# Block 1's mean and rate transposed inside a feature tile, block 2's two slots later, and block 3's statistics behind block 2's normalisation

## The chip, the cores and the metric

The kernel runs on one core of a Trainium2 chip. The metric is the device time of one execution, in microseconds (us); three executions are timed and their median counts. One further view, the profile, shows one of these executions instruction by instruction.

## The reference

The function takes x of 2048 rows and 512 columns, normalises every row, feeds the normalised rows to a 32-head attention and to a gated feed-forward network, and joins the two:

```python
def _layernorm(x, axis=-1, eps=1e-5):
    m = jnp.mean(x, axis=axis, keepdims=True)
    v = jnp.var(x, axis=axis, keepdims=True)
    return (x - m) / jnp.sqrt(v + eps)

def reference(A_x, A_wqkv, A_wo, B_x, B_w_gate, B_w_up, B_w_down):
    x = A_x
    xn = _layernorm(x, axis=-1)
    s = _A_ref(xn, A_wqkv, A_wo)                      # softmax attention, 32 heads of 16
    g = _silu(_B_ref(xn, B_w_gate, B_w_up, B_w_down)) # (silu(xn @ w_gate) * (xn @ w_up)) @ w_down
    return x + s * g
```

The change touches only the part that produces xn and its products with wqkv.

## The kernel before, in words

The 2048 rows are worked in four blocks (0 to 3) of 512 rows. The first 141.9 us are a prologue: xn of each block is made, split into two float32r halves (`hi` and `lo`, the tiles `xt`), and multiplied with wqkv. Then the attention runs with the feed-forward network's matmuls filled in between, to the end.

**Slots.** The prologue's matmuls are an explicit list of 48 slots, twelve to a block: slot number = 12 * block + position. A slot is one product tile of 12 matmuls on TensorE (PE). Eight slots of a block are *feature tiles* (`feature_tile`, line 770: queries and keys, 128 features by 512 rows), four are *value tiles* (`value_tile`, line 789). In blocks 0 and 1 the value tiles come first, in blocks 2 and 3 last. So slots 4 to 11 are block 0's feature tiles, 12 to 15 block 1's value tiles, 16 to 23 block 1's feature tiles, 24 to 31 block 2's feature tiles, 32 to 35 its value tiles, and block 3 begins at slot 36. A feature tile ends with a Square on ACT (line 775, into `sq`), a copy on ACT that rounds the high half (line 776, into `parts`), a subtraction on DVE for the low half (line 777), a store of 512 KB from SP (line 779) and, from block 1 on, a running maximum on DVE (line 781, `top`). The product's PSUM tile `ps` has four buffers, `parts` four and `sq` two.

**The normalised columns of blocks 1 to 3.** Block 0 is transposed by PE. The others are loaded twice: as rows for the statistics, and as columns (the transposed x, `A_x_columns`) for the normalisation. What has to be done for block b is cut into steps by `columns_of` (line 681), and each step is hung on a slot. The eight numbers of a call at lines 829 to 831 are the slots of: the load of the rows; the load of the columns (`turned`); the statistics (`counted`: BN_STATS and BN_AGGR, one pair per 128 rows; all four in one slot for block 1, two in each of two slots for blocks 2 and 3); the rate (`rated`: `rates_x`, nine small DVE operations and a square root on ACT that fill the tile `mr` with mean and rate); the transposition of `mr` (`spread`); the read of the result (`read`); the normalisation (`normed`: subtract and multiply on DVE with `wide_mr`, a rounding copy on ACT for `hi`); and the offsets of the low halves (`lows`).

`spread_mr` (line 673) is a chain over three engines: PE transposes `mr` into the PSUM tile `extra` (line 674), ACT copies it to SBUF (line 675), and ACT issues a DMA that writes the 4 KB to `mr_d` in HBM (line 676). `load_mr` (line 678) is the DMA from POOL's queue that reads `mr_d` and spreads it over all 128 partitions as `wide_mr` (512 KB). `store_x` (line 656) is a pair of 1 MB stores of a block's `xt` from POOL.

Nothing reorders the instructions: each engine takes them in the order in which the program writes them, and it waits at the first one whose inputs are not there. Steps of a slot marked 0 are written ahead of the slot's matmuls, those marked 1 behind its tile. The loop at line 837 calls `run_steps` for both.

`project` (line 711) writes the 12 matmuls of a tile, for each of four chunks c of the contraction: `hi` with the high weights, `lo` with the high weights, `hi` with the low weights. An `order` list may put another piece of work between them: an entry whose second part is `None` is called instead.

Of the kernel before, what the change touches and what calls it, by code (L numbers as in the profile page):

```python
# [28 lines left out]
DT = D // P  # L29
# [90 lines left out]
def tile_block(ctx: ExitStack, tc: tile.TileContext, x, xcols, wqkv, wo, w_gate, w_up, w_down, out):  # L120
# [401 lines left out]
    with ExitStack() as pro:  # L522
# [10 lines left out]
        xin = facc  # L533
# [15 lines left out]
        wh = pc.tile([P, 8, DT, P], F32R, name="wh")  # L549
        wl = pc.tile([P, 8, DT, P], F32R, name="wl")  # L550
# [51 lines left out]
        raw_x = pc.tile([P, DT, TB], F32, name="raw_x")  # L602
# [59 lines left out]
        def step(at, late, make, *what):  # L662
            steps.setdefault((at, late), []).append(partial(make, *what))
# [17 lines left out]
        def columns_of(b, rows, cols, ats):  # L681
            load, turned, counted, rated, spread, read, normed, lows = ats
            block = slice(b * TB, (b + 1) * TB)
            step(load, 0, sp.dma_start, rows, x[block].rearrange("(t p) d -> p t d", p=P))
            step(turned, 0, sp.dma_start, cols, xcols[:, block].rearrange("(c p) t -> p c t", p=P))
            for t in range(NT):
                step(counted + (t // 2 if b > 1 else 0), 0, stats, t, rows)
            step(rated, 0, rates_x)
            step(spread, 0, spread_mr, b)
            step(read, 1, load_mr, b)  # L690
            hi, lo = xt[b % 2]
            for t in range(NT if b == 1 else 0):
                of = slice(t * P, (t + 1) * P)
                raw = cols[:, :, of]
                step(normed + t + 1, 0, dve.tensor_sub, lo[:, :, of], raw, hi[:, :, of].bitcast(F32))
            for t in range(NT if b == 1 else 0):
                of = slice(t * P, (t + 1) * P)
                raw = cols[:, :, of]
                for i, change in enumerate((dve.tensor_sub, dve.tensor_mul)):
                    step(normed + t, 0, change, raw, raw, wide_mr[:, i, of][:, None].to_broadcast([P, DT, P]))  # L700
                step(normed + t, 1, nc.scalar.copy, hi[:, :, of], raw)
            for c in range(DT if b > 1 else 0):
                raw = cols[:, c]
                step(normed + c, 0, dve.tensor_sub, raw, raw, wide_mr[:, 0])
                step(normed + c, 0, dve.tensor_mul, raw, raw, wide_mr[:, 1])
                step(normed + c, 1, nc.scalar.copy, hi[:, c], raw)
                step(normed + lows[c], 1, dve.tensor_sub, lo[:, c], raw, hi[:, c].bitcast(F32))
            step(normed + lows[-1], 1, store_x, b)


        def project(pairs, xh, xl, tokens, order=None, ps=None):
            ps = ps or pps.tile([P, 512], F32, tag="ps", name="ps")
            n = 0
            terms = [((xh, whi), (xl, whi), (xh, wlo)) for whi, wlo, _ in pairs]
            for i, part in order or [(i, slice(0, 3)) for i in range(DT)]:
                if part is None:
                    i()
                    continue
                c = pairs[i][2]
                for a, w in terms[i][part]:  # L720
                    if tokens is None:
                        mm(ps, w, a[:, c], start=n == 0, stop=n == 3 * DT - 1)
                    else:
                        mm(ps, a[:, c, tokens], w, start=n == 0, stop=n == 3 * DT - 1)
                    n += 1
            return ps
# [42 lines left out]

        def feature_tile(b, m):  # L770
            xh, xl = xt[b % 2]
            ps = project([(wh[:, m, c], wl[:, m, c], c) for c in range(DT)], xh, xl, None)
            parts = p3.tile([P, 2, TB], F32R, tag="parts", name="parts")
            sq = p5.tile([P, TB], BF, tag="sq", name="sq") if b else top[m]
            act(sq, ps, AF.Square)
            nc.scalar.copy(parts[:, 0], ps)
            dve.tensor_sub(parts[:, 1], ps, parts[:, 0].bitcast(F32))
            dst = (q_d if m < 4 else k_d)[:, (m % 4) * P:(m % 4 + 1) * P, b * TB:(b + 1) * TB]
            sp.dma_start(dst.rearrange("s f t -> f s t"), parts.bitcast(F32))
            if b:  # L780
                dve.tensor_max(top[m], top[m], sq)
# [40 lines left out]
        def copy_fx(i):  # L822
# [4 lines left out]
            nc.scalar.copy(dst[:, 2 * w:2 * w + 2], xt[0][j][halves[u], 2 * w:2 * w + 2])  # L827

        columns_of(1, raw_x, xin, (1, 2, 2, 3, 5, 5, 9, (NT + 1,)))
        columns_of(2, raw_x, raw_x, (4, 11, 7, 9, 11, 14, 19, (1, 2, 3, 3)))  # L830
        columns_of(3, xin, raw_x, (16, 24, 17, 24, 26, 26, 31, (1, 2, 3, 3)))

        for b in range(NB):
            more = b + 1 < NB
            slots = [(feature_tile, m) for m in range(8)]
            slots = [(value_tile, t) for t in range(NT)] + slots if b < 2 else slots + [(value_tile, t) for t in range(NT)]
            for n, (make, i) in enumerate(slots):
# [60 lines left out]
        with tc.If(fast < 1):  # L898
            with tc.tile_pool(name="gen", bufs=1) as gen:
                for h in range(2):  # L900
                    pool.memset(qst[0][h * HALF:h * HALF + 2].bitcast(F32), 0.0)
                for g in range(NG):
                    for b in range(NB):
# [3 lines left out]
                        for j in range(NB):  # L907
                            load_k(g, j, j % 2)
                            for i in range(4 * NT):
                                h, t = divmod(i, NT)  # L910
                                ps = pps.tile([P, 512], F32, tag="ps", name="ps")
# [42 lines left out]
    for u in range(units):  # L954
        g, b = divmod(u, NB)
# [153 lines left out]
```

## Time and profile before

| | us |
|---|---|
| median of 3 executions (lowest, highest) | 1386.54 (1385.94, 1386.88) |
| the profiled execution's own time | 1385.94 |
| its span in the profile | 1384.2 |
| PE busy in the span | 1375.8 (99%) |
| ACT, DVE, POOL busy | 1157.0, 777.8, 104.7 |
| PE busy in the first 125 us | 121.46 |

The profiled execution took 1385.94 us by the clock that times all executions; 1384.2 us of that is the span from the first to the last instruction, and 1.74 us lie around it. A timeline row gives the start, the duration, the engine, the line, the operation with its output and input, and in square brackets how long the engine sat idle before and what released it. PEld is the weight load of PE; ACTq and SPq are DMA issues by those engines. Matmuls overlap: a row's duration is longer than the distance to the next matmul.

### The profile page before, as it was taken

Reading aid. Unit: us, or ns where it says so; the run is one execution under the profiler, and the core shown is the slowest. Engines: PE = TensorE matmul, PEld = TensorE weight load, DVE = VectorE, ACT = ScalarE, POOL = GpSimd, SP = SyncE. Lnnn points to the kernel's source line nnn. Section 1 sums busy time; section 2 is a strip of 40 time slices with the busy share of each in tenths; the row PEclk is TensorE's granted clock in tenths of the full one; section 3 lists DMA queues with packets and bytes.
Section 4 is the critical chain, followed back from the end, with each engine's and each line's share of the span. In section 5 each row is a group of like instructions: output and inputs, shape, how many; then the busy total and the mean of one; then the engine's idle time right before and its main releaser. Section 6 shows DMA issues by size and latency. Waiting matters only on the chain.

```text
span 1384.2 us, 27644 instructions
## 1 busy us (share of the span) xinstructions
PE 1375.8 (99%) x11152; PEld 866.4 (63%) x11152; DVE 777.8 (56%) x1256; ACT 1157.0 (84%) x1944; POOL 104.7 (8%) x148
## 2 busy tenths in 40 slices
PE   9999999999999999999999999999999999999998
PEld 7777666556655665565566555566566656656565
DVE  6565466365545663565465643655466545655656
ACT  6743589888888898899998988888888888899875
POOL 4300100000010000000110000000100000000142
PEclk9999999999999999999999999999999999999999
DMA  9889541124453511233724402256333312234752
GB/s 289 298 293 289 146 108 44 36 73 109 110 128 82 135 43 36 51 90 87 175 55 110 114 13 51 74 128 143 85 77 84 100 28 57 59 87 135 226 184 85
DMA packets 132900, 156.29 MB, mean 113 GB/s; under 512 B 13481, under 2 KB 83137, under 8 KB 131998
## 3 DMA queue, kind: packets, MB, share of 16 engines
q1 hardware_dynamic: 124974, 128.03, 35.5%
q0 software_dynamic: 7312, 25.89, 5.4%
q8 instruction: 89, 1.46, 0.4%
q10 hardware_dynamic: 480, 0.54, 0.1%
q14 instruction: 45, 0.37, 0.1%
HBM read 112.18 MB, written 40.12 MB: 110 GB/s over the span
## 4 chain that ended last, share of the span: by engine, by line
PE 89%; DVE 0%; DVEq 0%; issue 0%
PE acc L450 33%; PE bankx L244 30%; PE score L990 10%; PE single L990 8%; PE banky L244 6%; PE spare L990 1%; PE spare L1045 0%; PE banky L1045 0%; PE score L1045 0%; DVE y L1052 0%; PE single L1045 0%; DVE y L1058 0%; DVEq L1105 0%
## 5 line engine op out<-in xcount | busy, mean ns | idle before, releaser
L450 PE MATMUL acc<-pr,vst 128*17 128x512 f32 x4096 | 459.3, 593 | 0.0
L1000 ACT ACTIVATE pr<-single 128x512 f32<-128x512 f32 x762 | 429.4, 605 | 17.5 <-PE single L990 0.5
L993 ACT ACTIVATE pr<-score 128x1024 f32<-128x1024 f32 x318 | 327.9, 1031 | 87.5 <-PE score L990 84.6
L244 PE MATMUL bankx<-fx,guh 64*128 64x512 f32 x896 | 290.9, 392 | 0.1
L244 PE MATMUL banky<-fx,guh 64*128 64x512 f32 x896 | 290.9, 392 | 0.0
L450 PEld LDWEIGHTS acc<-pr,vst 128*17 128x17 f32 x4096 | 115.6, 97 | 279.4 <-issue 275.3
L997 DVE COPY pr<-spare 128x512 f32<-128x512 f32 x194 | 134.0, 691 | 183.4 <-PE spare L990 168.5
L990 PE MATMUL score<-qst,kst 50*128 50x512 f32 x830 | 218.6, 418 | 0.0
L990 PE MATMUL single<-qst,kst 50*128 50x512 f32 x922 | 212.4, 398 | 0.0
L244 PE MATMUL bankx<-wd,hh 64*128 64x512 f32 x672 | 196.0, 391 | 0.0
L244 PE MATMUL banky<-wd,hh 64*128 64x512 f32 x672 | 196.0, 391 | 0.0
L1010 ACT ACTIVATE pr<-pr 128x512 f32<-128x512 f32 x354 | 193.3, 641 | 0.0
L244 PEld LDWEIGHTS bankx<-fx,guh 64*128 64x128 f32 x896 | 166.8, 186 | 21.1 <-DVE guh L205 0.6
L244 PE MATMUL banky<-fx,gul 64*128 64x512 f32 x448 | 175.6, 392 | 0.0
L244 PE MATMUL bankx<-fx,gul 64*128 64x512 f32 x448 | 175.6, 392 | 0.0
L990 PEld LDWEIGHTS score<-qst,kst 50*128 50x128 f32 x830 | 98.7, 184 | 112.5 <-ACT pr L1000 68.8
L244 PEld LDWEIGHTS banky<-fx,guh 64*128 64x128 f32 x896 | 166.9, 186 | 0.4
L1000 ACT ACTIVATE pr<-score 128x512 f32<-128x512 f32 x194 | 117.0, 603 | 35.6 <-PE spare L990 26.7
L997 DVE COPY pr<-single 128x512 f32<-128x512 f32 x160 | 110.4, 690 | 58.8 <-PE single L990 47.8
L244 PEld LDWEIGHTS bankx<-wd,hh 64*128 64x128 f32 x672 | 125.1, 186 | 18.4
L990 PEld LDWEIGHTS single<-qst,kst 50*128 50x128 f32 x922 | 114.7, 184 | 23.5 <-ACT pr L1000 7.6
L244 PEld LDWEIGHTS banky<-wd,hh 64*128 64x128 f32 x672 | 125.1, 186 | 5.7
(195 smaller groups left out, 1688.9 us busy)
## 6 DMA issues: line engine op xcount, KB each, us to landing
gur<-in_B_w_gate_dram SPq DMA_DIRECT2D x56, 256.0 KB
gur<-in_B_w_up_dram SPq DMA_DIRECT2D x56, 256.0 KB
wdr<-in_B_w_down_dram SPq DMA_DIRECT2D x56, 256.0 KB
kst<-k_d SPq DMA_DIRECT2D x192, 64.0 KB
qst<-q_d SPq DMA_DIRECT2D x192, 64.0 KB
fx<-xt_d SPq DMA_DIRECT2D x24, 512.0 KB
q_d<-parts SPq DMA_DIRECT2D x16, 512.0 KB
k_d<-parts SPq DMA_DIRECT2D x16, 512.0 KB
```

Source lines behind the costliest of these rows:

```text
L244: mm(bank, lhs[h], rhs[h], start=start, stop=stop)
L450: mm(acc[h * 32:h * 32 + DH + 1], v[:, kt % CT, h * (DH + 1):(h + 1) * (DH + 1)], probs[2 * i + h // 2][:, h % 2], start=kt == 0, stop=kt ...
L990: mm(banked[h], k[r, j, kc * P:(kc + 1) * P], q[r, j], start=True, stop=True)
L993: exps.append(act(pr, both_banks, AF.Exp, scale=0.25))
L997: dve.tensor_copy(pr[:, h], banked[h])
L1000: exps.append(act(pr[:, h], banked[h], AF.Exp, scale=0.25))
L1010: exps.append(act(part, part, AF.Exp, scale=0.25))
```

## The change

Three edits, in four lines of the table and two functions. Block 1's `spread_mr` is no longer called ahead of slot 5 but from inside that slot's feature tile (block 0, m = 1), behind two of its four chunks, which is six matmuls later. Block 2's `spread_mr` goes from slot 11 to slot 13, and the read of its result from slot 14 to slot 13. For block 3 the load of the rows goes from slot 16 to 18, the statistics from slots 17 and 18 to 23 and 24, the rate from 24 to 25, and transposition and read from 26 to 27. Sizes and counts of all instructions stay the same.

```diff
             step(rated, 0, rates_x)
-            step(spread, 0, spread_mr, b)
+            if b > 1:
+                step(spread, 0, spread_mr, b)
             step(read, 1, load_mr, b)
...
         def feature_tile(b, m):
             xh, xl = xt[b % 2]
-            ps = project([(wh[:, m, c], wl[:, m, c], c) for c in range(DT)], xh, xl, None)
+            order = [(c, slice(0, 3)) for c in range(DT)]
+            if (b, m) == (0, 1):
+                order.insert(2, (partial(spread_mr, 1), None))
+            ps = project([(wh[:, m, c], wl[:, m, c], c) for c in range(DT)], xh, xl, None, order)
...
-        columns_of(2, raw_x, raw_x, (4, 11, 7, 9, 11, 14, 19, (1, 2, 3, 3)))
-        columns_of(3, xin, raw_x, (16, 24, 17, 24, 26, 26, 31, (1, 2, 3, 3)))
+        columns_of(2, raw_x, raw_x, (4, 11, 7, 9, 13, 13, 19, (1, 2, 3, 3)))
+        columns_of(3, xin, raw_x, (18, 24, 23, 25, 27, 27, 31, (1, 2, 3, 3)))
```

The diff adds a line and then three more, so line 777 of before is line 781 of after, and so on. In the rows that follow, `xt_167` and `xt_168` are the high and low halves of blocks 0 and 2, `xt_169` and `xt_170` those of blocks 1 and 3.

PE at the start of slot 11, before: the transposition of block 2's mean and rate stands ahead of the last feature tile of block 0.

```order
L722 MATMUL ps<-xt_168,wh 128x512
L722 MATMUL ps<-xt_167,wl 128x512
L674 MATMUL extra<-ident,mr 8x128
L722 MATMUL ps<-xt_167,wh 128x512
L722 MATMUL ps<-xt_168,wh 128x512
```

PE after, at the start of slot 13:

```order
L725 MATMUL ps<-vh,xt_170 128x512
L725 MATMUL ps<-vl,xt_169 128x512
L674 MATMUL extra<-ident,mr 8x128
L725 MATMUL ps<-vh,xt_169 128x512
L725 MATMUL ps<-vh,xt_170 128x512
```

It moved by 24 matmuls, and now stands between two value tiles of block 1.

POOL behind the last weight split, before (`kst` and `qst` are attention tiles that get a constant; slots 11 to 15):

```order
L881 MEMSET qst_566 2x1024 x2
L658 DMA xt_d<-xt_169 128x2048
L658 DMA xt_d<-xt_170 128x2048
L679 DMA wide_mr<-mr_d 128x1024
L785 DMA v_d<-vt 128x8x272
```

POOL after:

```order
L885 MEMSET qst_563 2x1024 x2
L679 DMA wide_mr<-mr_d 128x1024
L658 DMA xt_d<-xt_169 128x2048
L658 DMA xt_d<-xt_170 128x2048
L789 DMA v_d<-vt 128x8x272
```

The load of block 2's mean and rate went ahead of the two 1 MB stores of block 1's xn.

DVE in slots 17 to 19, before: two pairs of block 3's statistics (from `facc`, where its rows lie) stand ahead of block 2's first normalisation (`raw_x` with `wide_mr`); two more pairs stand just above.

```order
L777 TENSOR_TENSOR parts<-ps,parts 128x512
L781 TENSOR_TENSOR top_155<-top_155,sq 128x512
L611 BN_STATS st<-facc 128x6
L612 BN_AGGR mv<-st 128x2
L611 BN_STATS st<-facc 128x6
L612 BN_AGGR mv<-st 128x2
L777 TENSOR_TENSOR parts<-ps,parts 128x512
L781 TENSOR_TENSOR top_156<-top_156,sq 128x512
L667 TENSOR_TENSOR raw_x<-raw_x,wide_mr 128x512 x2
```

DVE after, in slots 22 and 23:

```order
L781 TENSOR_TENSOR parts<-ps,parts 128x512
L785 TENSOR_TENSOR top_160<-top_160,sq 128x512
L667 TENSOR_TENSOR xt_168<-raw_x,xt_167 128x512 x2
L611 BN_STATS st<-facc 128x6
L612 BN_AGGR mv<-st 128x2
L611 BN_STATS st<-facc 128x6
L612 BN_AGGR mv<-st 128x2
L781 TENSOR_TENSOR parts<-ps,parts 128x512
L785 TENSOR_TENSOR top_161<-top_161,sq 128x512
```

The statistics now stand behind the last two low halves of block 2 (`xt_168<-raw_x,xt_167`).

## The prediction

> **What bounds the kernel now.** First the page: its busy table says which engine to look at. Then the waits of PE over the whole span, and PE's timeline around the two that matter.
>
> ```profile
> span 1384.2 us, 27644 instructions
> ...
> PE 1375.8 (99%) x11152; PEld 866.4 (63%) x11152; DVE 777.8 (56%) x1256; ACT 1157.0 (84%) x1944; POOL 104.7 (8%) x148
> ```
>
> ```profile
> PE extra L674 <- DVE mr L629: 1.4, 1, 1.4
> ...
> PE ps L722 <- DVE xt L667: 1.0, 1, 1.0
> ```
>
> ```profile
> 39.66 0.40 PE L722 MATMUL ps<-xt,wl 128*128 128x512 f32 x1
> 41.45 0.27 PE L674 MATMUL extra<-ident,mr 128*8 128x128 f32 x1 [1.40 <-DVE mr L629]
> ...
> 44.35 0.63 PE L724 MATMUL ps<-vh,xt 128*128 128x512 f32 x2
> ...
> 77.95 0.63 PE L722 MATMUL ps<-xt,wh 128*128 128x512 f32 x2
> ...
> 78.65 0.63 PE L722 MATMUL ps<-xt,wh 128*128 128x512 f32 x2
> ...
> 79.35 0.40 PE L722 MATMUL ps<-xt,wh 128*128 128x512 f32 x1
> 80.79 0.50 PE L722 MATMUL ps<-xt,wh 128*128 128x512 f32 x1 [1.05 <-DVE xt L667]
> ```
>
> PE is busy 99% of the span: what keeps it waiting is paid in full, and other engines' work counts only where PE waits for it. The list of PE's waits has one more row, at the kernel's opening, which the change leaves alone. The two shown are in its reach: the transposition of block 2's `mr` at slot 11, and block 2's first feature tile (slot 24, from 77.95), which stops for a low half.
>
> The distance between matmuls gives their true price. Three take 78.65 - 77.95 = 0.70 us, one 0.233. Slot 12 starts at 44.35 and slot 24 at 77.95, so a slot is 33.60 / 12 = 2.80 us. At slot 11 the transposition was due at 39.66 + 0.23 = 39.89 and came at 41.45: **1.56 us lost**. In slot 24 the matmul due at 79.35 + 0.23 = 79.58 came at 80.79: **1.21 us lost**. Together 2.77.
>
> **Part 1, block 1's transposition inside slot 5.**
>
> ```profile
> 23.05 0.27 PE L674 MATMUL extra<-ident,mr 128*8 128x128 f32 x1
> ```
>
> ```profile
> 24.73 0.25 ACT L675 COPY busy<-extra 8x128 f32<-8x128 f32 x1
> 25.01 0.59 ACTq L676 DMA_DIRECT2D mr_d<-busy  x1
> ```
>
> ```profile
> 36.81 1.42 DVE L667 TENSOR_TENSOR facc<-facc,wide_mr 128x512 f32<-128x512 f32 x2 [0.49 <-DMA wide_mr<-mr_d]
> ```
>
> PE had no idle time here in before, and the transposition costs it the same in the new place: six matmuls (1.40) later, at about 24.5, ending near 24.8. ACT came to it only at 24.73, so the chain slips by 0.1 us or so. DVE waits for that chain (0.49 at 36.81) and hands the slip on. Cost on PE: between 0 and 0.1, taken as 0, with part 2's spare as cover.
>
> **Part 2, block 2's transposition at slot 13.** The 1.56 goes: `mr` is done just before 41.45, and PE reaches slot 13 two slots later. What is late next is block 1's own low halves, which PE now wants 1.56 earlier.
>
> ```profile
> 41.92 0.68 DVE L667 TENSOR_TENSOR xt<-facc,xt 128x512 fp32r<-128x512 f32 x1
> ...
> 47.92 0.69 DVE L667 TENSOR_TENSOR xt<-facc,xt 128x512 fp32r<-128x512 f32 x1 [0.68 <-ACT xt L667]
> ...
> 50.63 0.69 DVE L667 TENSOR_TENSOR xt<-facc,xt 128x512 fp32r<-128x512 f32 x1 [0.69 <-ACT xt L667]
> ```
>
> ```profile
> 44.49 0.25 ACT L675 COPY busy<-extra 8x128 f32<-8x128 f32 x1
> 44.77 0.28 ACTq L676 DMA_DIRECT2D mr_d<-busy  x1
> 45.09 0.60 ACT L775 ACTIVATE top<-ps 128x512 bf16<-128x512 f32 x1 [0.35 <-ACT busy L675]
> ```
>
> Slot 12 starts at 44.35 - 1.56 = 42.79; its second matmul, at 43.02, reads the first low half, done at 41.92 + 0.68 = 42.60. Slot 14 (48.39, its second matmul 48.62) reads the third, done at 48.61 in before; slot 15 (51.19, 51.42) the fourth, done at 51.32. Before both, DVE waited for ACT, and on ACT the copy and the DMA issue of `mr` (44.49 to 45.09, 0.6 us) now stand behind that work. So they come at about 48.0 and 50.7: spare 0.4, 0.6 and 0.7 us. If ACT gives nothing back it is 0.4, 0.0 and 0.1. New wait: 0 to 0.4, taken as 0.1.
>
> On POOL the load of `wide_mr` now waits for `mr_d` ahead of two 1 MB stores.
>
> ```profile
> 29.78 0.57 POOL L679 DMA_DIRECT2D wide_mr<-mr_d  x1 [3.57 <-DMA mr_d<-busy]
> ```
>
> ```profile
> 86.34 0.27 ACTq L676 DMA_DIRECT2D mr_d<-busy  x1
> ```
>
> ```profile
> 93.65 0.54 POOL L679 DMA_DIRECT2D wide_mr<-mr_d  x1 [11.48 <-DMA mr_d<-busy]
> ```
>
> ```profile
> DMA to landing us min/median/max: 7.0/7.1/12.0
> ```
>
> ACT's issue of `mr_d` now stands behind block 1's last high half (for which DVE waited until 50.63), at about 50.1. The first hop took 29.78 - 25.01 = 4.8 for block 1 and 93.65 - 86.34 = 7.3 us for block 3; the second, in the row of landings (the transfers of `wide_mr`), 7.0 to 12.0. So `wide_mr` lands between 50.1 + 4.8 + 7.0 = 61.9 and 50.1 + 7.3 + 12.0 = 69.4. The 12.0 must be block 2's, which stood behind 2 MB of stores: block 1's was read at 36.81 and block 3's at 102.75, each less than 10 us from its issue. Now it goes ahead, so I take the low end, 62. The stores wait a few us longer; nothing in the prologue reads them.
>
> [...]
>
> **Part 3, block 3's statistics behind block 2's normalisation.**
>
> ```profile
> 51.34 0.37 SPq L667 DMA_DIRECT2D facc<-in_A_x_dram  x1
> ```
>
> ```profile
> 59.65 0.69 DVE L777 TENSOR_TENSOR parts<-ps,parts 128x512 fp32r<-128x512 f32 x1 [8.34 <-ACT parts L776]
> ...
> 64.73 0.69 DVE L611 BATCH_NORM_STATS2 st<-facc 128x6 f32<-128x512 f32 x1 [4.06 <-DMA facc<-in_A_x_dram]
> ...
> 65.56 0.66 DVE L611 BATCH_NORM_STATS2 st<-facc 128x6 f32<-128x512 f32 x1
> ...
> 69.81 1.41 DVE L667 TENSOR_TENSOR raw_x<-raw_x,wide_mr 128x512 f32<-128x512 f32 x2
> ...
> 77.80 1.41 DVE L667 TENSOR_TENSOR raw_x<-raw_x,wide_mr 128x512 f32<-128x512 f32 x2
> 79.12 0.68 DVE L777 TENSOR_TENSOR parts<-ps,parts 128x512 fp32r<-128x512 f32 x1
> ...
> 80.06 1.28 DVE L667 TENSOR_TENSOR xt<-raw_x,xt 128x512 fp32r<-128x512 f32 x2
> ...
> 82.19 0.16 DVE L670 COPY mr<-mv 128x4 f32<-128x4 f32 x1
> ...
> 83.39 0.17 DVE L629 SCALAR_TENSOR_TENSOR mr<-nw,mr 128x4 f32<-128x4 f32 x1
> ...
> 102.75 1.41 DVE L667 TENSOR_TENSOR raw_x<-raw_x,wide_mr 128x512 f32<-128x512 f32 x2
> ...
> 111.50 0.69 DVE L667 TENSOR_TENSOR xt<-raw_x,xt 128x512 fp32r<-128x512 f32 x1 [0.61 <-ACT xt L667]
> ```
>
> ```profile
> 48.00:64.00 16.00, 16.00 (x71) 12.86 (x70) 3.62 (x6) 10.76 (x15) 2.53 (x4) 1.00 1.01 363
> 64.00:80.00 16.00, 15.74 (x68) 12.34 (x66) 14.99 (x30) 10.83 (x18) 0.00 (x0) 1.00 0.60 226
> ```
>
> DVE stood 4.06 us at block 3's rows and from there hardly paused (14.99 busy in the 16 us from 64, the third busy figure) until the low half that PE waited for: slot 24's stall comes from there. Four pairs of statistics (65.56 - 64.73 = 0.83 each, 3.3 us) and the wait for their rows leave the way. Block 2's normalisation is then bound by its slot. Tile 16's subtraction came at 59.65, 1.3 us after slot 17 began (44.35 + 5 x 2.80); tile 18's so comes at 62.4 + 1.3 = 63.7, and with its maximum DVE is free at 64.6. Four normalisations (79.12 - 77.80 = 1.32), four tiles' subtraction and maximum (80.06 - 79.12 = 0.94) and four low halves (0.64) make 11.6 us, and some 1.1 of waiting for tiles 19 and 20: done at 77.3. Slot 24 starts at 76.39 and wants the last two low halves at 78.0 and 78.7: 1.2 us or more of spare, so 1.21 is gained.
>
> The statistics follow: four pairs (3.3), two tiles (1.9) and the rate (83.56 - 82.19 = 1.4) give `mr` at 83.9; slot 27 wants it at 76.39 + 8.40 = 84.8. The rows' load is issued near 62, behind tile 17's store, and took 13.4 us in before (51.34 to 64.73): 75.5, in time for 77.3. DMA engines were full from 48 to 64 and 60% busy from 64 to 80 (the last figure but one), so this megabyte, some 3 us at 363 GB/s, fits. Block 3's chain, a slot later on a PE 2.77 earlier, keeps the old 86.3 and lands at 86.3 + 7.3 + 7.1 = 100.7. From 102.75 to the last low half's end are 9.4 us, 0.6 of it a wait that shortens with PE; slot 36 (77.95 + 1.21 + 33.60 - 2.77 = 110.0) wants that half at 112.4. So the normalisation may start as late as 103.6. Cost 0, with 1 to 3 us of cover.
>
> **Sum.** 1.56 + 1.21 - 0.1 = 2.67 us off the profiled execution: 1385.94 - 2.67 = 1383.27. It was the fastest of three, the median is 0.60 above. The removed waits hang on transfers and PE's other work hardly waits, so part of the 0.60 is likely these waits grown longer; I take half: 1386.54 - 2.67 - 0.30 = **1383.6**. With 0.4 of new wait and none of the 0.60 it is 1384.2; with no new wait and all of it 1383.2, and 0.4 of scatter (half of the three runs' 0.94) below that 1382.8. A measurement of this kernel can tell about 0.2%, 2.77 us, from no change: a line at 1383.77, just above the forecast.
>
> **The rivals.**
> *Block 1's low halves take the wait's place* at slots 12 to 15. For it: spare of 0.4, none if DVE's chain slips. Against: ACT's shorter queue. A slip of 1 us gives 1384.3.
> *Block 2's mean and rate land too late.* DVE has 1.1 us of waits and 1.2 behind them, so a landing after 66.9 stops slot 24. At the upper end, 69.4, that is 2.5 us: gain 0.5, 1386.1. Against: the load now stands first.
> *Block 3 becomes the stop* (slower). The same two hops, DMA engines full, at slot 36: from a normalisation start of 103.6 PE pays one for one. Both hops at 12.0 give 86.3 + 24.0 + 0.5 = 110.8, 7.2 us, less the 2.94 gained: 1390.8. It is slower than before from 106.5. Against: in before that load was read at 102.75 without a wait.
> *The edits do nothing*, because another product of DVE is as late at both places: 1386.5. No row shows one.
>
> **How the numbers follow.** Forecast 0.66, block 1's halves 0.11, block 2 late 0.08, block 3 late 0.13, nothing 0.02. About three quarters of the forecast lie below 1383.77, as its sum was made from the fastest execution: faster 0.49. Same: 0.17 + 0.11 + 0.08 + 0.02 = 0.38. Slower 0.13. The range 1382.8 to 1386.3 leaves out block 3 late and the last case; the forecast's own is 1382.8 to 1384.2.
>
> **What would show it.** Right: L674 without idle time at slot 13; no PE wait for `xt` near 78; no DVE wait for block 3's rows. Wrong: a PE wait between 42 and 52, DVE waiting for `wide_mr` past 66.9, or PE waiting for `mr` near 85 or for `xt` near 110 to 113.

## The result, and the profile after

The changed kernel took 1383.37 us (median of 12 executions, 1382.67 to 1385.37) against 1386.63 (12 executions, 1385.72 to 1388.81) of the kernel before: 3.26 us less, a ratio of 0.9976 with a 95% interval of 0.9968 to 0.9985. The forecast was 1383.6, the range 1382.8 to 1386.3. Run again beside three of the experiments it was 2.46 us faster (0.9982, 0.9973 to 0.9991).

The page's head and the list of PE's waits after the change (us in total, times, longest):

```profile
span 1382.0 us, 27647 instructions
...
PE 1375.3 (100%) x11152; PEld 866.1 (63%) x11152; DVE 777.8 (56%) x1256; ACT 1157.3 (84%) x1944; POOL 105.1 (8%) x148
```

```profile
PE extra L579 <- DVE ind L586: 1.1, 1, 1.1
PE acc L639 <- DVE xn L737: 0.5, 1, 0.5
PE ps L761 <- DMA wraw<-in_A_wqkv_dram: 0.2, 1, 0.2
```

Both waits in the change's reach are gone; the three rows left belong to the opening (before 8.2 us). PE's busy time did not shrink (1375.8 to 1375.3): the span is shorter by idle time alone. This execution's opening was slower than that of the profile before: PE was busy 18.18 us of its first 20 against 18.90, so the rows below stand about 0.45 us late for a reason outside the change. From slot 9 on they stand about 0.75 us late: slot 8 lost another 0.3 us, which part 1 below comes back to.

PE's timeline at the transposition of slot 13, and at slot 24, which starts at 77.09:

```profile
46.00 0.39 PE L725 MATMUL ps<-vl,xt 128*128 128x512 f32 x1
46.23 0.27 PE L674 MATMUL extra<-ident,mr 128*8 128x128 f32 x1
...
77.09 0.63 PE L723 MATMUL ps<-xt,wh 128*128 128x512 f32 x2
...
78.49 0.63 PE L723 MATMUL ps<-xt,wh 128*128 128x512 f32 x2
...
79.19 0.63 PE L723 MATMUL ps<-xt,wh 128*128 128x512 f32 x2
```

The transposition follows its predecessor by the usual 0.23. In slot 24 chunks three and four (78.49 and 79.19) come at the pace of 0.70 per three matmuls. DVE, ACT, POOL and SP, which set what PE finds:

```profile
50.43 0.69 DVE L667 TENSOR_TENSOR xt<-facc,xt 128x512 fp32r<-128x512 f32 x1 [0.69 <-ACT xt L667]
...
65.38 1.41 DVE L667 TENSOR_TENSOR raw_x<-raw_x,wide_mr 128x512 f32<-128x512 f32 x2
...
77.50 1.29 DVE L667 TENSOR_TENSOR xt<-raw_x,xt 128x512 fp32r<-128x512 f32 x2
78.70 0.69 DVE L611 BATCH_NORM_STATS2 st<-facc 128x6 f32<-128x512 f32 x1
...
84.98 0.16 DVE L629 SCALAR_TENSOR_TENSOR mr<-nw,mr 128x4 f32<-128x4 f32 x1
...
99.31 1.42 DVE L667 TENSOR_TENSOR raw_x<-raw_x,wide_mr 128x512 f32<-128x512 f32 x2 [0.17 <-DMA wide_mr<-mr_d]
```

```profile
50.58 0.27 ACTq L676 DMA_DIRECT2D mr_d<-busy  x1
...
75.94 0.59 ACT L780 CAST parts<-ps 128x512 fp32r<-128x512 f32 x1 [0.79 <-DMA q_d<-parts]
```

```profile
54.65 0.57 POOL L679 DMA_DIRECT2D wide_mr<-mr_d  x1 [9.03 <-DMA mr_d<-busy]
55.21 1.07 POOL L658 DMA_DIRECT2D xt_d<-xt  x2
```

```profile
62.72 1.27 SPq L667 DMA_DIRECT2D facc<-in_A_x_dram  x1
```

And the two windows that the prediction shows of before, now after the change (DMA share is the last figure but one), with the landings of `wide_mr`:

```profile
48.00:64.00 16.00, 16.00 (x70) 12.93 (x69) 4.45 (x8) 11.38 (x18) 2.53 (x4) 1.00 0.81 279
64.00:80.00 16.00, 16.00 (x70) 12.87 (x69) 13.79 (x25) 11.44 (x18) 1.08 (x2) 1.00 1.05 351
```

```profile
DMA to landing us min/median/max: 4.8/6.5/7.0
```

Block 2's normalisation starts at 65.38, 4.4 us earlier than before, and PE no longer overtakes it. Note POOL: it now stands 9.03 us at the load of `wide_mr`, and block 1's two stores of 1 MB leave at 55.21 instead of 50.89. POOL before, for comparison:

```profile
50.89 0.57 POOL L658 DMA_DIRECT2D xt_d<-xt  x1 [5.67 <-ACT xt L667]
51.62 0.53 POOL L658 DMA_DIRECT2D xt_d<-xt  x1 [0.16 <-issue]
52.14 0.53 POOL L679 DMA_DIRECT2D wide_mr<-mr_d  x1
```

The DMA engines' full stretch comes later than before (0.81, then 1.05; before 1.01, then 0.60). The experiments show that the moved stores are more than a side effect.

### The profile page after: what moved, and what is told of

Its sections match the earlier page's. It is cut to its first block, busy times and chain, and to the rows that moved or that the text cites. A ratio compares the mean times of both kernels' runs of the same rounds, so it can differ in the third digit from the quotient of the medians.

```text
span 1382.0 us, 27647 instructions
## 1 busy us (share of the span) xinstructions
PE 1375.3 (100%) x11152; PEld 866.1 (63%) x11152; DVE 777.8 (56%) x1256; ACT 1157.3 (84%) x1944; POOL 105.1 (8%) x148
## 4 chain that ended last, share of the span: by engine, by line
PE 89%; DVE 0%; DVEq 0%; issue 0%
PE acc L450 33%; PE bankx L244 29%; PE score L994 10%; PE single L994 8%; PE banky L244 7%; PE spare L994 1%; PE spare L1049 0%; PE banky L1049 0%; PE single L1049 0%; DVE y L1056 0%; PE score L1049 0%; DVE y L1062 0%; DVEq L1109 0%
```

## The experiments

Each kernel was timed beside the kernel before, in the same session; the times are differences of the medians, with the ratio and its interval.

**1. Block 1's edit alone.**

```diff
-        columns_of(2, raw_x, raw_x, (4, 11, 7, 9, 13, 13, 19, (1, 2, 3, 3)))
-        columns_of(3, xin, raw_x, (18, 24, 23, 25, 27, 27, 31, (1, 2, 3, 3)))
+        columns_of(2, raw_x, raw_x, (4, 11, 7, 9, 11, 14, 19, (1, 2, 3, 3)))
+        columns_of(3, xin, raw_x, (16, 24, 17, 24, 26, 26, 31, (1, 2, 3, 3)))
```

> Only block 1's transposition goes inside slot 5; blocks 2 and 3 as before. Theory: PE had no wait there and the chain behind it slips by 0.1 us, so the time stays within 0.5 us of before, and both PE waits (1.4 and 1.0 us in the list) stay. Rival: the edit shortens block 1's chain by itself and takes over 0.5 us off.

Measured: -0.13 us, 1.0000 (0.9991 to 1.0009). PE's waits in its profile:

```profile
PE ps L723 <- DVE xt L667: 1.4, 1, 1.4
...
PE extra L674 <- DVE mr L629: 0.7, 1, 0.7
```

Both waits are there, 0.7 and 1.4 instead of 1.4 and 1.0. A shorter first stop brings PE to the second one earlier, so the two may trade between executions; two profiles do not show that. The edit is worth nothing that can be measured.

**2. Block 2's edit alone** (the kernel before, with the one line of the table).

```diff
-        columns_of(2, raw_x, raw_x, (4, 11, 7, 9, 11, 14, 19, (1, 2, 3, 3)))
+        columns_of(2, raw_x, raw_x, (4, 11, 7, 9, 13, 13, 19, (1, 2, 3, 3)))
```

> Only block 2's transposition and read go to slot 13. Theory: the wait at slot 11 goes (1.56 us), but slot 24 waits for a chain that is held by the landing of block 3's rows and not by PE, so PE only arrives there earlier and waits 1.2 + 1.5 = about 2.7 us instead of 1.2; the time falls by 0 to 0.8 us. Rival: the two waits are independent and the time falls by 1.4 to 1.8 us with the wait of slot 24 still near 1.2.

Measured: -2.71 us, 0.9983 (0.9974 to 0.9992), and no PE wait on `mr` or `xt`. Both expectations fell: this edit alone gives what all three give, as far as the intervals can tell. Its profile, DVE at block 3's first statistics (still in slot 17) and POOL:

```profile
59.75 0.69 DVE L611 BATCH_NORM_STATS2 st<-facc 128x6 f32<-128x512 f32 x1
```

```profile
56.18 0.57 POOL L679 DMA_DIRECT2D wide_mr<-mr_d  x1 [10.69 <-DMA mr_d<-busy]
56.74 1.06 POOL L658 DMA_DIRECT2D xt_d<-xt  x2
```

DVE does not wait for the rows any more (4.06 us before). Their load was issued at 51.01, as before; what changed is that POOL's two stores, held behind the load of `wide_mr`, left at 56.74 instead of 50.89. That became the new theory, for runs 5 and 6.

**3. Block 3's edit alone** (the kernel before, with the other line).

```diff
-        columns_of(3, xin, raw_x, (16, 24, 17, 24, 26, 26, 31, (1, 2, 3, 3)))
+        columns_of(3, xin, raw_x, (18, 24, 23, 25, 27, 27, 31, (1, 2, 3, 3)))
```

> Only block 3's load, statistics, rate, transposition and read move. Theory: the wait at slot 11 stays at 1.4 to 1.6 us, the one in slot 24 goes; time 1.0 to 1.5 us below before. Rival: the two waits are linked in this direction too and the time hardly falls.

Measured: -1.64 us, 0.9990 (0.9981 to 0.9999). As the theory had it, slot 24's wait is gone and slot 11's stays; the gain is a little over the 1.0 to 1.5 us expected, well within the interval:

```profile
PE extra L674 <- DVE mr L629: 1.6, 1, 1.6
```

**4. Blocks 2 and 3, without the edit inside slot 5** (both lines above in the kernel before).

> Both table edits without the one inside slot 5. Theory: block 1's edit is worth nothing, so the time falls by 2.7 to 3.3 us as in the whole change and no wait for mr or xt is left on PE. Rival: block 1's place matters, a wait between 42 and 52 us shows, and the fall is 0.4 us or more smaller.

Measured: -2.69 us, 0.9983 (0.9974 to 0.9992), no PE wait for `mr` or `xt`. It cannot be told from run 2: on top of block 2's edit, block 3's adds nothing that can be measured, and block 1's neither.

**5. Block 2's transposition moved, its read not** (the kernel before, one number).

```diff
-        columns_of(2, raw_x, raw_x, (4, 11, 7, 9, 11, 14, 19, (1, 2, 3, 3)))
+        columns_of(2, raw_x, raw_x, (4, 11, 7, 9, 13, 14, 19, (1, 2, 3, 3)))
```

> The second edit without its read: block 2's transposition at slot 13, but the load of wide_mr back at slot 14, behind the two 1 MB stores of block 1; the rest as before. Theory now: the second edit also cured slot 24, because its load waits for mr_d ahead of those stores and so keeps them off the DMA engines while block 3's rows come in. With the stores first again (issued near 51 us) the rows land near 64 us, slot 24 waits about 2.7 us, and the time is within 0.8 us of before. Rival: the shorter wait at slot 11 alone lets DVE be in time; then the time is again 2.7 us below before and no wait for xt shows.

Measured: +2.59 us, 1.0017 (1.0008 to 1.0026): slower than before, though slot 11's wait is gone. The mechanism of the theory was there, its time (within 0.8 us) was missed. POOL, SP, DVE and PE in its profile:

```profile
50.19 0.57 POOL L658 DMA_DIRECT2D xt_d<-xt  x1 [5.07 <-ACT busy L675]
```

```profile
50.65 0.37 SPq L667 DMA_DIRECT2D facc<-in_A_x_dram  x1
```

```profile
65.69 0.69 DVE L611 BATCH_NORM_STATS2 st<-facc 128x6 f32<-128x512 f32 x1 [6.25 <-DMA facc<-in_A_x_dram]
```

```profile
77.41 0.40 PE L722 MATMUL ps<-xt,wh 128*128 128x512 f32 x1
78.90 0.50 PE L722 MATMUL ps<-xt,wh 128*128 128x512 f32 x1 [1.09 <-DVE xt L667]
...
79.47 0.40 PE L722 MATMUL ps<-xt,wh 128*128 128x512 f32 x1
81.77 0.57 PE L722 MATMUL ps<-xt,wh 128*128 128x512 f32 x1 [1.90 <-DVE xt L667]
82.13 0.63 PE L722 MATMUL ps<-xt,wl 128*128 128x512 f32 x1
...
85.12 0.80 PE L722 MATMUL ps<-xt,wh 128*128 128x512 f32 x2
```

With the stores first again the rows hold DVE until 65.69, and the wait that left slot 11 comes back at slot 24: 78.90 - 77.41 - 0.23 = 1.26 and 81.77 - 79.47 - 0.23 = 2.07, in all 3.33 us against 2.77 before. That is 0.56 of the 2.59 us. More of the loss is in the windows, whose last figure but two is the granted clock:

```profile
80.00:82.00 2.00, 0.23 (x1) 0.23 (x2) 2.00 (x5) 1.79 (x4) 0.54 (x1) 1.00 0.26 94
82.00:84.00 2.00, 2.00 (x6) 1.56 (x6) 1.96 (x9) 0.00 (x0) 0.53 (x1) 0.52 1.03 371
84.00:86.00 2.00, 2.00 (x8) 1.56 (x7) 1.26 (x5) 1.07 (x2) 0.00 (x0) 0.63 1.02 397
86.00:88.00 2.00, 2.00 (x11) 1.54 (x10) 0.26 (x1) 0.36 (x1) 0.00 (x0) 1.00 0.99 404
```

After two gaps close together the granted clock was 0.52 and 0.63 for two windows of 2 us, with 1.00 in the windows on either side: the seven matmuls from 82.13 to 85.12 took 2.99 us instead of 7 x 0.233 = 1.63, another 1.4. What set the dip off was not shown: the gaps were 1.26 and 2.07 us, and three matmuls ran between them. The profile of the kernel before, with gaps of 1.56 and 1.21 us far apart, kept 1.00.

The eleven executions of this run fit. One had a mean granted clock of 1.000 on record and took 1386.90 us, 0.59 above the kernel before, which is the 0.56 of the gaps and within the theory's 0.8. The other ten had 0.998 or 0.999 and took 1388.43 to 1390.10.

**6. Only block 1's stores later** (the kernel before).

```diff
-            step(normed + lows[-1], 1, store_x, b)
+            step(normed + lows[-1] + (2 if b == 1 else 0), 1, store_x, b)
```

> Only block 1's two 1 MB stores from POOL go two slots later (slot 14 to 16); all else as before. Theory: block 3's rows land by about 60 us, DVE no longer waits 4 us for them, slot 24's wait (1.2 us) goes and slot 11's (1.5) stays: 1.0 to 1.5 us below before. Rival: the stores do not hold up the rows; DVE waits for them until about 64 as before and the time is unchanged.

Measured: -1.64 us, 0.9986 (0.9977 to 0.9995). PE's remaining wait, POOL and DVE:

```profile
PE extra L674 <- DVE mr L629: 1.3, 1, 1.3
```

```profile
57.77 1.07 POOL L658 DMA_DIRECT2D xt_d<-xt  x2
```

```profile
60.82 0.69 DVE L611 BATCH_NORM_STATS2 st<-facc 128x6 f32<-128x512 f32 x1
```

No wait of DVE for the rows, no wait of slot 24. The edit also lets the load of `wide_mr` go ahead of the stores (50.44 instead of 52.14), but DVE waited for the rows before, not for `wide_mr`. Runs 5 and 6 together show it: slot 24's stall came from block 1's 2 MB of stores and block 3's 1 MB of rows on the DMA engines at the same time, with block 3's statistics ahead of block 2's normalisation on DVE: DVE stood 4.06 us at the rows before, 6.25 in run 5 and not at all in run 6.

**7. The whole change once more.**

> The whole change once more, beside the next three. Theory: 2.5 to 3.3 us below before, no PE wait for mr or xt; it is no better than the second edit alone was (-2.7 us).

Measured: -2.46 us, 0.9982 (0.9973 to 0.9991), just under the 2.5 expected and within the interval of run 2.

**8. The whole change with block 2's read back behind the stores.**

```diff
-        columns_of(2, raw_x, raw_x, (4, 11, 7, 9, 13, 13, 19, (1, 2, 3, 3)))
+        columns_of(2, raw_x, raw_x, (4, 11, 7, 9, 13, 14, 19, (1, 2, 3, 3)))
```

> The whole change, but the load of wide_mr back at slot 14, behind block 1's two 1 MB stores. Without the third edit this order cost 2.6 us over before. Theory: with block 3's rows and statistics out of the way DVE does not stand still for them, so the order of stores and load no longer matters; wide_mr lands by 66.9 us, and the time is within 0.8 us of the whole change (2.5 to 3.3 below before). Rival: the load behind the stores lands after 66.9, slot 24 waits and the time is 1 us or more above the whole change.

Measured: -3.22 us, 0.9977 (0.9968 to 0.9986), no PE wait for `xt`. The order that cost 2.59 us in run 5 costs nothing that can be measured once block 3's statistics stand behind the normalisation, and `wide_mr` behind the stores lands in time:

```profile
54.27 0.54 POOL L679 DMA_DIRECT2D wide_mr<-mr_d  x1 [2.88 <-DMA mr_d<-busy]
```

```profile
DMA to landing us min/median/max: 6.6/6.7/7.3
```

With block 3's rows not yet on their way, no landing took over 7.3 us, against 12.0 before: 54.27 + 7.3 = 61.6 at the latest.

**9. The whole change with block 3's rows loaded at slot 16 again.**

```diff
-        columns_of(3, xin, raw_x, (18, 24, 23, 25, 27, 27, 31, (1, 2, 3, 3)))
+        columns_of(3, xin, raw_x, (16, 24, 23, 25, 27, 27, 31, (1, 2, 3, 3)))
```

> The whole change, but the load of block 3's rows back at slot 16. Theory: it was the place of the statistics on DVE and of the stores on POOL that mattered, not the slot of this load; the time is within 0.8 us of the whole change and no PE wait for xt shows. Rival: the earlier megabyte delays wide_mr past 66.9 or the tile stores, and slot 24 waits by 0.5 us or more.

Measured: -3.04 us, 0.9979 (0.9970 to 0.9988), no PE wait. The slot of that load does not matter by itself.

**10. Block 3's transposition and read three slots later still**, to measure the cover.

```diff
-        columns_of(3, xin, raw_x, (18, 24, 23, 25, 27, 27, 31, (1, 2, 3, 3)))
+        columns_of(3, xin, raw_x, (18, 24, 23, 25, 30, 30, 31, (1, 2, 3, 3)))
```

> The whole change, with block 3's transposition and read three slots later still (27 to 30). It measures the cover that the prediction gave block 3: the normalisation may start as late as about 104 us. Here mr_d would be issued near 96 and wide_mr land near 108. Theory: PE waits 3 to 6 us for xt at slot 36, and the time is that much above the whole change, above before too. Rival: the cover is larger than worked out, and the time is within 1 us of the whole change.

Measured: +1.78 us against before, 1.0012 (1.0003 to 1.0021), so 4.24 above the whole change of the same session. DVE and PE's waits:

```profile
107.15 1.42 DVE L667 TENSOR_TENSOR raw_x<-raw_x,wide_mr 128x512 f32<-128x512 f32 x2 [8.52 <-DMA wide_mr<-mr_d]
```

```profile
PE ps L725 <- DVE parts L781: 1.6, 1, 1.6
PE ps L723 <- DVE xt L667: 1.2, 2, 1.0
```

The normalisation started at 107.15, 3 us past the limit of about 104, and PE waited 2.8 us; by the distance between matmuls the three gaps cost 1.77, 0.38 and 1.13, in all 3.3 us. But the larger part is not the wait for `xt` at slot 36: DVE, standing 8.52 us at `wide_mr`, held up a tile's subtraction behind it, and PE ran out of product buffers first. The 4.24 holds more than this. The profiled execution took 1386.74, 1.35 below the median of its run, and the four longest of the eleven (1389.33 to 1390.65) had a mean granted clock of 0.997 or 0.998.

The program is that of the whole change up to slot 26, and its profile shows something at slot 24 that the list of PE's waits leaves out, as it is a weight load (PEld) that waits for block 2's low half:

```profile
78.19 0.19 PEld L723 LDWEIGHTS ps<-xt,wh 128*128 128x128 f32 x1 [0.49 <-DVE xt L667]
```

PE lost 0.3 us there (slot 24 took 3.12 us instead of 2.80).

## Why the prediction was right or wrong

*Part 1* held as far as times can tell: the edit inside slot 5 is worth nothing measurable (run 1, and run 4 against run 7, intervals of over a microsecond each way). But its chain reaches PE by a path that was not named. POOL waits for `mr_d` at the load of `wide_mr`, and behind that load stands a weight split whose result (`wl`) slot 8 needs:

```profile
30.71 0.57 POOL L679 DMA_DIRECT2D wide_mr<-mr_d  x1 [4.04 <-DMA mr_d<-busy]
31.30 2.55 POOL L574 TENSOR_TENSOR wl<-wraw,wh 128x512 fp32r<-128x512 f32 x2
```

```profile
32.66 0.19 PEld L723 LDWEIGHTS ps<-xt,wl 128*128 128x128 f32 x1 [0.47 <-POOL wl L574]
```

Slot 8 took 3.09 us in this profile instead of 2.80, more than the "between 0 and 0.1" of the prediction. A wait of a weight load for `wl` shows only in the two profiles of the whole change (0.47, and 0.24 in run 7, where PE lost 0.06), where the first hop took 5.2 and 5.0 us; in the other ten it took 4.7 to 4.9. Whether the edit's slip or the slower hop is to blame was not tried.

*Part 2*, the 1.56 us of slot 11, held, and so did the working of what comes next. The last low half of block 1 came at 50.43 (from 50.63 before, though PE was about 0.75 late by then, from the opening and slot 8); PE waited in none of slots 12 to 15, so the 0.1 of new wait was 0. The first hop took 54.65 - 50.58 = 4.1 us, less than either bound from the rows (4.8, 7.3); the landing, at 61.7 at the latest, met the 62 that was taken.

*The step that failed* is the sentence that the stores "wait a few us longer; nothing in the prologue reads them". Nobody reads them, but they moved: in runs 2 and 6, where block 3's rows are still loaded near 51, keeping 2 MB off the DMA engines for 6 to 7 us more (56.74 and 57.77 instead of 50.89) is what let the rows in. So the time was right and its attribution was not. The 1.21 us of slot 24 were credited to block 3's edit; either edit removes them alone (runs 2 and 3), and with block 2's in place block 3's adds nothing that can be measured.

*Part 3* held in its cause (DVE's stop at block 3's rows) and in its outcome, with less cover than worked out. Block 2's last low half ended at 77.50 + 1.29 = 78.79 and was wanted at 77.09 + 10 x 0.233 = 79.42: 0.6 us instead of 1.2, since ACT stood 0.79 us at a tile's store (75.94) that came late. The later stores fit as its cause: with the DMA engines at 1.05 here and at 1.04 in run 10 ACT stood there 0.79 and 1.49 us, and in run 10 the cover was gone; in run 8, where the stores go first and the engines are at 0.86, ACT does not stand there, and the half ends 1.4 us ahead. So the sentence on the stores missed a cost too, of up to 0.3 us. `mr` of block 3 was ready at 85.14 and PE's transposition at slot 27 followed without idle time. The normalisation began at 99.31, where 103.6 was the limit; run 10, which started 3 us past it and lost 3.3, bears out a limit near 104.

*The 0.30 us added for the median* has no support. The whole change, its repetition and the four variants without a PE wait (runs 2, 4, 8, 9) lie between -2.46 and -3.26, with a mean of -2.9 and intervals of over a microsecond each way. That does not tell 2.67 from 2.97. Run 1's profile, with waits of 0.7 and 1.4 instead of 1.4 and 1.0, lends no support to the reason given. PE's slots show what the sum left out. From the start of slot 9 to that of slot 11 PE took 7.16 us before (34.32 to 41.48) and 5.57 after (35.09 to 40.66), and in slot 24 it took 4.12 (77.95 to 82.07) and 2.80 (77.09 to 79.89): the two stops were worth 1.59 + 1.32 = 2.91 us, not 2.67. The 0.1 of new wait did not come, the matmul behind a stop came 0.34 before the next one instead of 0.233 (80.79 and 81.13 before), and a few hundredths lie around the moved transposition. That the 0.30 nearly makes up for these 0.24 is luck.

*The rivals.* None happened to the change as it is. "Block 3 becomes the stop" is real and was brought about in run 10, by one mechanism more than named (product buffers). The small stops of slots 8 and 24 are not among them. Not foreseen was a slower case in the change itself: had block 2's read stayed at slot 14 without block 3's edit, it would have been 2.59 us slower than before (run 5, without the edit inside slot 5).

## What to carry to other kernels

Removing a wait of the busiest engine helps only as far as the next thing it meets is paced by that engine too; where the next thing hangs on a transfer, the engine arrives earlier and waits longer (run 5: slot 11's 1.56 us went, and slot 24 lost 3.33 us instead of 1.21). When a load is moved ahead of stores in a queue, ask what the delayed stores were colliding with, not only who reads them (run 2: block 1's left 5.85 us later, and DVE's 4.06 us at block 3's rows were gone). Where two edits each cure the same stall, time each alone before crediting either.

## What was not expected of the hardware

Gaps of 1.26 and 2.07 us in PE's work, three matmuls apart, were followed by a granted clock of 0.52 and 0.63 over the next two windows of 2 us, and cost another 1.4 us; the gaps of 1.56 and 1.21 us of the kernel before, 39 us apart, left it at 1.00. So a PE wait is not always paid one for one. Run 10's gaps (1.77, 0.38 and 1.13 us, up to 4 us apart) left it at 1.00 in the profile too. The same kernel can go either way: one of eleven executions of run 5 kept a mean of 1.000, four of eleven of run 10 fell to 0.997 or 0.998, and so did four of the 87 executions of the kernel before that were timed beside the experiments (0.998; 1388.86 to 1389.47 us, all among the five longest). What decides it was not tried.
